# RWKV-5 attention with a tanh-shrink MLP: the upper halves of the loads issued from other queues, and a planner that counts SBUF ports

## The chip, the cores and the metric

The kernel runs on one core of a Trainium2 chip. The metric is the device time of one execution in microseconds (us); lower is better. The time before is 605.67 us, the median of three runs (603.26, 605.67 and 606.02).

## The reference

The inputs are `r`, `k`, `v` of shape (4, 8, 768, 48), that is batch, heads, sequence and head width, in float32; `w` and `u` of shape (8, 48); and two weight matrices, `w_in` (384, 2048) and `w_out` (2048, 384), which arrive in float64.

```python
state = np.zeros((B, H, D, D), dtype=np.float32)
for t in range(S):
    kt, vt, rt = (k[:, :, t], v[:, :, t], r[:, :, t])
    cur = np.einsum('bhd,bhe->bhde', u[None] * kt, vt)
    y[:, :, t] = np.einsum('bhd,bhde->bhe', rt, state + cur)
    state = w[None, :, :, None] * state + np.einsum('bhd,bhe->bhde', kt, vt)
x = y.transpose(0, 2, 1, 3).reshape(B * S, H * D)      # 3072 x 384
h = x @ w_in
g = h - np.tanh(h)
out = (g @ w_out).astype(np.float32)
```

## The kernel before

**Attention.** The recurrence is computed in chunks of 64 steps. A `unit(n)` is one chunk of two batches: the first batch lies on partitions 0 to 63, the second on partitions 64 to 127 (`HALF[0]` and `HALF[1]`). There are 24 units. Each loads its `r`, `k` and `v` in `fetch` (line 745): six DMAs, one for each tensor and each half `z`, of 64 partitions x 8 heads x 48 numbers, 96 KB in 512 runs of 192 bytes. All of these are issued by SyncE (SP) at line 750, the first half and then the second. A unit's tiles come from rings of three buffers, so that the load of unit n has to wait until unit n - 3 has been read. A unit then transposes r and k on TensorE (PE, line 763), scales them (VectorE, lines 767 and 894), multiplies them (`levels`, `from_state`, `outputs`, PE line 717), copies a masked part (VectorE, line 919) and updates the state (VectorE, lines 882 and 928). ScalarE (ACT) writes the diagonal (line 788) and the outputs `xt` and `rest` (line 855). Two units make a block of 256 tokens; when its second unit is done, GpSimd (POOL) issues six small DMAs that fill the remaining rows of `xt` from `rest` (line 876).

**Weights.** They arrive in float64, and are converted to float32 on the chip. There are 16 pieces, in turn two of `w_in` and two of `w_out`, each 768 KB in float64. `Weights.load` (line 123) brings a piece into one of four staging tiles `st`; `convert` takes five VectorE and two ScalarE instructions (lines 137 to 143). A `w_out` piece is a single SP DMA over 128 partitions. A `w_in` piece is four DMAs, because its rows are rearranged: 48 main rows (288 KB, 144 runs of 2 KB) and 16 other rows (96 KB, 48 runs) for partitions 0 to 63, and the same for partitions 64 to 127. SP issues the two main parts, POOL the two small ones.

**Dense.** There are 12 blocks of 8 tiles each. A tile is `h = x @ w_in` for 256 hidden columns (12 PE instructions, line 168), the activation (five on ScalarE, lines 177 to 185, and four on VectorE, lines 192 to 198), and the second product. For 25 tiles (24 early ones and the very last) the product is written directly (`o`, line 206). After all the weights have been converted and mixed (`mixing`, line 266), the other 71 tiles take a form with seven products instead of eight (`p`, line 257), with sums on POOL (lines 242 to 246).

**Order.** The order of instructions on every engine is not written by hand. Every step is a task of `Plan`, with an engine, a cost in us, what it comes after and, for a DMA, `data`: how long it holds the transfer channel. `forward` lays out the tasks with these costs, engine by engine, and gives a makespan. `order` searches: it starts from due times found backwards, jitters due times at random, and keeps what does not lengthen the plan; first with a plan cut off at `BUSY` us, then with the whole plan. The tasks are then issued in order of their planned start. Each engine and each DMA queue works through its own instructions in that order, so an instruction that waits holds up those behind it. A weight load is `gated`: it does not start before 9.5 us (`FIRST`) in the plan. The plan keeps a DMA off a queue that has eight in flight (`LANES`).

Of the kernel before, what the change touches and what calls it, by code (L numbers as in the profile page):

```python
# [33 lines left out]
AHEAD = 2  # L34
# [266 lines left out]
class Plan:  # L301
# [6 lines left out]

    HOP, NEAR_HOP, LANDS, LANDED, LANES, EARLY, SPARE, WARM, SLOW = 0.16, 0.06, 2.4, 1.6, 8, 45.0, 20.0, 6.0, (60.0, 3.0)
    AHEAD, BUSY = 0.05, 240.0  # L310
    CHUNK, CHUNK_0, ASKED, COMES, FIRST = 256, 192, 55, 3.4, 9.5
# [4 lines left out]

    def add(self, engine, cost, run, after=(), due=1e9, data=0, gated=False, steps=0):
        t = SimpleNamespace(engine=engine, cost=cost, run=run, after=[x for x in after if x], due=due, data=data,
                            gated=gated, steps=steps, then=[], n=len(self.tasks))
        for x in t.after:  # L320
            x.then.append(t)
        self.tasks.append(t)
        return t
# [12 lines left out]
    def forward(self, due, until=1e9):  # L336
# [3 lines left out]
        waiting = self.queues(ready, count)  # L340
        free, lanes, channel = dict(self.BEGIN), {}, 0.0
        step, bound, comes, fills = 0, self.CHUNK_0, 0.0, iter(self.fills)
# [3 lines left out]
        while len(done) < len(ready):  # L346
# [40 lines left out]
            if t.data:  # L387
                channel = max(channel, start + 1.2) + t.data
                end = max(end + self.LANDS, channel + self.LANDED) + self.slow(start)
                lanes[e] = lanes[e][1:] + [end]  # L390
# [58 lines left out]

    def order(self, first=2500, tries=500):  # L450


        due = [t.due for t in self.tasks]
        for t in reversed(self.tasks):
            for x in t.then:
                due[t.n] = min(due[t.n], due[x.n] - t.cost - self.HOP - (self.LANDS if t.data else 0))
        plan = self.forward(due)
        for _ in range(4):
            due = self.backward(plan)
            plan = self.forward(due)  # L460
        chance = Random(5)

        def moved():
            by, at, wide = chance.choice((0.3, 1, 2, 5)), chance.uniform(0, until), chance.choice((15, 40, 100, 700))
            return [x + chance.gauss(0, by) * (start is not None and abs(start - at) < wide / 2) for x, start in zip(due, plan[1])]


        until = self.BUSY
        plan = self.forward(due, until)
        for _ in range(first):  # L470
            new = moved()
            other = self.forward(new, until)
            if other[0] <= plan[0]:
                plan, due = other, new
        plan = self.forward(due)
        until = plan[0]
        for _ in range(tries):
            new = moved()
            other = self.forward(new)
            if chance.random() < .5:  # L480
                latest = self.backward(other)
                again = self.forward(latest)
                if again[0] < other[0]:
                    other, new = again, latest
            if other[0] <= plan[0]:
                plan, due = other, new
# [29 lines left out]
def near(ctx, tc, r, k, v, w, u, out, shared, moe_w_in, moe_w_out):  # L516
# [136 lines left out]
    def fills(to):  # L653
# [20 lines left out]
    doubled = add("ACT", .6, lambda: A.copy(twice, inverse[:, :, None, 1:].to_broadcast([128, NP, 2, SHORT])), [now])  # L674
    now = tabled = add("PE", .7, table, [doubled], steps=8)
    downs = add("ACT", .5, lambda: A.copy(w_down, tab.rearrange("s (h d) -> s h d", h=H)[:, :, :D]), [now])
# [6 lines left out]
        out=ub.rearrange("p h d -> p (h d)"),  # L683
        in_=bass.AP(tensor=u.tensor, offset=u.offset, ap=[[0, 128], [1, H * D]])), data=.7)

# [15 lines left out]
    for n in range(weights.count):  # L701

        queues, data = (("SP",), (3.0,)) if n % 4 > 1 else (("SP", "POOL") * 2, (1.2, .95) * 2)
        of = [add(e, .55, lambda n=n, i=i, e=e: weights.load(n, i, e_of[e]), [converted[n - 4] if n >= 4 else None],
                  data=x, gated=True) for i, (e, x) in enumerate(zip(queues, data))]
        if weights.sources[n % 4 > 1].dtype != I64:
            converted.append(of[-1])
            continue
        step = steps(lambda n=n: weights.convert(n))
        now = of + ([converted[n - 2]] if n >= 2 else [])  # L710
        for name, cost in (("DVE", .47), ("DVE", .47), ("ACT", .84), ("ACT", .84), ("DVE", .87), ("DVE", .87), ("DVE", .87)):
            now = [add(name, cost, step, now)]
        converted += now
# [7 lines left out]
    def unit(n):  # L721
# [21 lines left out]
        direct = j == 0  # L743

        def fetch(name, src, after):
            def run(z):
                if name == "k" and not hasattr(t, "kt"):
                    t.kt = first_k[slot] if direct else load.tile([128, H, D], F32, name="kt", tag="kt")
                to = {"r": rt, "v": vt}.get(name)
                Q.dma_start(out=(t.kt if to is None else to)[HALF[z], :, :D],  # L750
                            in_=src[half * 2 + z, :, steps_at, :].rearrange("h t d -> t h d"))

            of = [add("SP", .65, lambda z=z: run(z), after, data=.71) for z in range(2)]
            return add("none", 0, lambda: None, of)
# [135 lines left out]
        if two:  # L890
            free = [b1.xt, b1.rest, b1.add, b1.cp, b1.diag]
        turns, turned = .46, 16
        x.turn = add("PE", turns, lambda: turn(rt, r_ps), [x.r] + free, steps=turned)
# [9 lines left out]
        if product:  # L903
            now = add("ACT", 1.05, own_k, [x.kT, w_us])
            x.own = add("PE", .7, own_levels, [now, x.rT, b2.out], steps=64)
            x.diag = add("DVE", .64, lambda: V.copy_predicated(t.at, same.bitcast(I32)[:, None, None, :].to_broadcast([128, 2, NP, SHORT]), own_lev), [x.own, b2.out])
# [7 lines left out]
        if two:  # L914
            now = add("PE", .66, from_state, both + [x.rT, b1.xt, b1.rest, b1.add, b2.decay, x.kT], steps=64)
            begun = [add("ACT", .15, between, [now])]
        x.lev = add("PE", .7 if two else (1.33 if swap else 1.73) if ch else .7, levels,
                    begun + [x.kT, x.rT, b2.out] + ([b2.decay, b1.xt, b1.rest, b1.add] if ch else []), steps=128 if ch and not two else 64)
        x.cp = add("DVE", .64, lambda: V.copy_predicated(t.at, before, lev), [x.lev, b2.out] + ([] if product else [x.diag]))  # L919
        x.out = now = add("PE", .95 if direct else 1.21, outputs,  # L920
                          [x.cp, x.diag, x.v, b1.xt, b1.rest, b1.add] + ([x.extra] if direct else [x.kw]), steps=96 if direct else 128)
        if direct:
            now = x.out = add("PE", .55, to_state, [now, x.kw], steps=64)
        x.xt = add("ACT", .96 if swap else .4, to_xt, [now, last_h.get(j - FIRST - 2) if slot == 0 else None])
        if not direct:
            x.rest = add("ACT", .62 if swap else .26, to_rest, [x.xt] + (filled.get((j - 2, "all"), []) if slot == 0 else []))
        x.add = add("DVE" if ch else "ACT", .47 if ch else 1.2, keep, [x.out, x.rest, x.xt]) if more else None
        x.decay = x.add if not ch else add("DVE", .47, lambda: V.tensor_tensor(state[:, :, :, :D], state[:, :, :, :D], w_all, ALU.mult), [x.add]) if more else None
        if direct:
            filled.setdefault((j, "all"), []).append(x.xt)  # L930
        elif slot == L - 1:
            filled[j, "all"] = [add("POOL", .52, lambda i=i, kk=kk: fill(i, kk), [x.rest, x.xt], data=.1)
                                for kk in range(NK) for i in range(2)]
# [17 lines left out]
    def finished_seven(t, x, half, due, pace):  # L951
# [9 lines left out]
        for i in (1, 0):  # L961
            now = steps[4 if i else 6]
            if t.fs[0]:
                now = add("DVE", .47, lambda i=i: dense.gather(t, i), [now], due + 3 * pace)
            stored[j, i] = [add("POOL", .6, lambda z=z, i=i: dense.store(t.os[i], L * j + i, z, G), [now], due + 4 * pace, data=.4)
                            for z in range(2)]

    def hidden(j, fs, f, due, pace, seven=False):
# [40 lines left out]
        for i in range(L):  # L1009
# [7 lines left out]
            if whole and j < d.NB - 1:  # L1017

                stored[j, i] = [add("POOL", .6, lambda z=z, i=i, ends=ends: dense.store(ends.o, L * j + i, z, G),
                                    [x.empty[-1]], due + 4 * pace, data=.4) for z in range(2)]  # L1020

# [339 lines left out]
```

## Time and profile before

| What | Value |
|---|---|
| median of three runs | 605.67 us |
| profiled execution | 607.26 us |
| its span, first to last instruction | 605.5 us |
| mean granted TensorE clock | 0.989 |
| TensorE busy | 582.4 us (96%) |
| VectorE busy | 466.4 us (77%) |
| ScalarE busy | 403.3 us (67%) |
| GpSimd busy | 201.0 us (33%) |
| packets of the DMA queue of SP (q1) | 81084, 25.57 MB |
| packets of the DMA queue of POOL (q0) | 4992, 6.99 MB |

The page of a profile splits the span into 40 slices of 15.1 us, and gives for each engine a digit for its busy share in tenths. The chain of work that ended last is followed back from the last instruction through whatever released each step. A table of windows gives the busy time of an engine in stretches that one chooses, the granted clock, the mean share of the time for which the 16 DMA engines had a packet under way, and the rate at which bytes moved. The name SPq means the sequencer of SP, which does no work but issue DMAs. Matmul ends are modelled, so a busy TensorE may still be fed slowly.

### The profile page before, as it was taken

The numbers are of one execution on the slowest core, as the hardware profiler recorded it, in microseconds if no ns is written. First come the engines' busy times: TensorE is split into PE (matmuls) and PEld (weight loads), VectorE is DVE, ScalarE is ACT, GpSimd is POOL, SyncE is SP. The second block draws the span as 40 slices with busy tenths as digits, with TensorE's granted clock in tenths as the row PEclk, the third lists the DMA queues.
The fourth block names the chain that finished last, engine by engine and source line by source line (L and its number), as shares of the span: only waits on it lengthen the run. The fifth ranks groups of instructions, "written<-read, shape, count | busy, mean of one in ns | idle before, by whom it ended". The sixth has DMA issues, their size and how long they took to land.

```text
span 605.5 us, 14670 instructions
## 1 busy us (share of the span) xinstructions
PE 582.4 (96%) x5781; PEld 485.7 (80%) x5781; DVE 466.4 (77%) x782; ACT 403.3 (67%) x902; POOL 201.0 (33%) x366
## 2 busy tenths in 40 slices
PE   8877999999999999999999999999999999999996
PEld 4555767667777669999999999888889889889995
DVE  6699699999999999867677776767765775555666
ACT  3677699899866676655556686465866676565652
POOL 5002212021000123544455473425334435334540
PEclk9889899999999999999999999999999999999999
DMA  6966585967300210110111020122201100100101
GB/s 125 228 126 126 113 194 99 143 167 124 105 14 0 48 28 14 26 27 1 28 27 26 2 60 1 41 41 48 53 16 34 41 2 8 29 2 8 26 3 30
DMA packets 86326, 33.78 MB, mean 56 GB/s; under 512 B 78536, under 2 KB 80680, under 8 KB 86248
## 3 DMA queue, kind: packets, MB, share of 16 engines
q1 hardware_dynamic: 81084, 25.57, 21.1%
q0 software_dynamic: 4992, 6.99, 5.5%
q8 instruction: 47, 0.77, 0.5%
q14 instruction: 31, 0.25, 0.2%
q10 hardware_dynamic: 172, 0.20, 0.1%
HBM read 26.94 MB, written 4.72 MB: 52 GB/s over the span
## 4 chain that ended last, share of the span: by engine, by line
PE 76%; DVE 6%; DMA 5%; ACT 4%; issue 4%; SPq 3%; POOL 1%; DVEq 0%; ACTq 0%; POOLq 0%
PE h L168 37%; PE p L257 26%; PE o L206 6%; PE yk_ps L717 4%; SPq L750 3%; DMA st<-in_moe_w_in_dram 2%; DMA xt<-rest 1%; PE yk_ps L763 1%; POOL xt L876 1%; DMA st<-in_moe_w_out_dram 1%; DVE rT L767 1%; DVE at L919 1%; ACT s L177 1%; DVE tg L194 1%; DVE g L198 1%
## 5 line engine op out<-in xcount | busy, mean ns | idle before, releaser
L168 PE MATMUL h<-xt,w_in_sb 128*128 128x256 f32 x1152 | 285.7, 385 | 2.7 <-DMA xt<-rest 2.7
L168 PEld LDWEIGHTS h<-xt,w_in_sb 128*128 128x128 f32 x1152 | 214.6, 192 | 35.9 <-issue 2.1
L242 POOL TENSOR_TENSOR sg<-g 128x256 f32<-128x256 f32 x69 | 52.1, 755 | 176.7 <-DVE g L198 152.2
L257 PE MATMUL p<-mixed,sg 128*128 128x192 f32 x426 | 104.1, 326 | 0.0
L192 DVE TENSOR_TENSOR g<-h,th 128x512 f32<-128x512 f32 x96 | 65.8, 686 | 48.9 <-ACT s L177 23.0
L194 DVE SCALAR_TENSOR_TENSOR tg<-s,tg 128x512 f32<-128x512 f32 x96 | 71.1, 741 | 36.6 <-ACT tg L181 20.0
L181 ACT ACTIVATE tg<-h 128x512 f32<-128x512 f32 x96 | 57.2, 596 | 58.5 <-PE h L168 56.9
L179 ACT ACTIVATE th<-h 128x512 f32<-128x512 f32 x96 | 57.4, 598 | 39.1 <-PE h L168 39.0
L177 ACT ACTIVATE s<-h 128x512 f32<-128x512 f32 x96 | 57.4, 598 | 37.3 <-PE h L168 37.2
L876 POOL DMA_DIRECT2D xt<-rest x66 | 32.5, 499 | 146.3 <-ACT rest L855 145.8
L257 PEld LDWEIGHTS p<-mixed,sg 128*128 128x128 f32 x426 | 75.0, 190 | 0.3 <-issue 0.3
L198 DVE COPY_PREDICATED g<-small,tg 128x512 f32<-128x512 int32 x96 | 71.1, 741 | 4.7 <-DVE tg L196 0.5
L257 PE MATMUL p<-w_out_sb,g 128*128 128x192 f32 x284 | 71.9, 335 | 1.1 <-DVE at L919 1.1
L196 DVE SCALAR_TENSOR_TENSOR tg<-q,tg 128x512 f32<-128x512 f32 x96 | 67.5, 703 | 6.4 <-ACT q L183 2.4
L206 PE MATMUL o<-w_out_sb,g 128*128 128x384 f32 x192 | 71.3, 495 | 0.1
L183 ACT ACTIVATE q<-s,m1b 128x512 f32<-128x512 f32 x96 | 69.8, 727 | 0.6
L185 ACT ACTIVATE small<-s,smallb 128x512 f32<-128x512 f32 x96 | 69.6, 725 | 0.3
L257 PEld LDWEIGHTS p<-w_out_sb,g 128*128 128x128 f32 x284 | 51.8, 190 | 9.0 <-DVE at L919 1.5
L788 ACT ACTIVATE at<-same,du 128x64 f32<-128x64 f32 x184 | 47.9, 343 | 2.8 <-DVE du L784 2.6
L206 PEld LDWEIGHTS o<-w_out_sb,g 128*128 128x128 f32 x192 | 35.2, 190 | 15.8 <-DVE g L198 0.2
L246 POOL TENSOR_TENSOR sg<-sg,g 128x128 f32<-128x128 f32 x69 | 41.0, 594 | 5.1
L244 POOL TENSOR_TENSOR sg<-sg,g 128x128 f32<-128x128 f32 x69 | 36.6, 530 | 5.2
(133 smaller groups left out, 672.3 us busy)
## 6 DMA issues: line engine op xcount, KB each, us to landing
st<-in_moe_w_out_dram SPq DMA_DIRECT2D x8, 768.0 KB, 4.5
rt<-in_r_dram SPq DMA_DIRECT2D x48, 96.0 KB, 2.9
vt<-in_v_dram SPq DMA_DIRECT2D x48, 96.0 KB, 3.4
st<-in_moe_w_in_dram SPq DMA_DIRECT2D x16, 288.0 KB, 5.5
kt<-in_k_dram SPq DMA_DIRECT2D x44, 96.0 KB, 3.1
out_dram<-o POOLq DMA_DIRECT2D x44, 96.0 KB, 2.2
st<-in_moe_w_in_dram POOLq DMA_DIRECT2D x16, 96.0 KB, 6.0
xt<-rest POOLq DMA_DIRECT2D x66, 16.0 KB, 2.1
```

The lines of the kernel that those rows point to most:

```text
L168: self.nc.tensor.matmul(t.h2[:, z], self.w_in_sb[:, t.f // 2, kk, z * 128 : (z + 1) * 128], self.xts[t.j][:, kk].rearrange("p b t -> p (b ...
L177: A.activation(out, t.h, AF.Square)
L179: A.activation(out, t.h, AF.Tanh)
L181: A.activation(out, t.h, AF.Tanh, scale=G1)
L183: A.activation(out, t.s, AF.Square, bias=self.m1b)
L185: A.activation(out, t.s, AF.Relu, bias=self.smallb, scale=-1.0)
L192: V.tensor_tensor(t.g, t.h, t.th, ALU.subtract)
L194: V.scalar_tensor_tensor(t.tg, t.s, C4, t.tg, ALU.mult, ALU.mult)
L196: V.scalar_tensor_tensor(t.tg, t.q, K1, t.tg, ALU.add, ALU.mult)
L198: V.copy_predicated(t.g, t.small.bitcast(I32), t.tg)
L206: self.nc.tensor.matmul(self.outs[i], t.g2[:, z, i * C : (i + 1) * C], self.w_out_sb[:, t.f + z, :], start=t.first and z == 0, stop=t.last ...
L257: self.nc.tensor.matmul(ps[bank][:, half * n : (half + 1) * n], a, b, start=t.first and half == 0, stop=t.last, skip_group_check=True)
```

## The change

It has two parts.

The first moves DMAs between queues. Of a `w_in` piece, the main rows for partitions 64 to 111 go from SP to POOL, and the small part for partitions 112 to 127 from POOL to SP. Of the loads of r, k and v, the second batch (partitions 64 to 127) is issued by ACT for units 0 and 1, by POOL for units 2 to 11, and by SP as before from unit 12 on.

The second changes the planner. A task with `side` 0 or 1 also occupies a port group for 1.75 times its channel time; every queue has its own ring; many costs are given other numbers; the first search is cut off at 110 us instead of 240, and is done four times with 2000 tries, of which the best is kept; the search over the whole plan has 300 tries instead of 500. Since the order of every engine comes out of this search, it can differ everywhere.

```diff
-    HOP, ..., LANDS, LANDED, LANES, EARLY, SPARE, WARM, SLOW = 0.16, 0.06, 2.4, 1.6, 8, 45.0, 20.0, 6.0, (60.0, 3.0)
-    AHEAD, BUSY = 0.05, 240.0
+    HOP, ..., LANDS, LANDED, LANES, EARLY, SPARE, WARM, SLOW = 0.16, 0.06, 2.1, 1.35, 8, 45.0, 20.0, 6.0, (60.0, 1.5)
+    AHEAD, BUSY, STARTS = 0.05, 110.0, 4
+    HALF = 1.75
...
             if t.data:
-                channel = max(channel, start + 1.2) + t.data
-                end = max(end + self.LANDS, channel + self.LANDED) + self.slow(start)
+                begin = max(start + 1.4, ring.get(e, 0.0))
+                channel = max(channel, begin) + t.data
+                ring[e] = channel
+                if t.side is not None:
+                    ports[t.side] = max(ports[t.side], begin) + self.HALF * t.data
+                    ring[e] = max(channel, ports[t.side])
+                end = max(end + self.LANDS, ring[e] + self.LANDED) + self.slow(start)
...
-    def order(self, first=2500, tries=500):
+    def order(self, first=2000, tries=300):
...
-        for _ in range(first):
-            new = moved()
...
+        until, begun, best = self.BUSY, due, None
+        for _ in range(self.STARTS):
+            due = begun
+            plan = self.forward(due, until)
+            for _ in range(first):
...
+            if best is None or plan[0] < best[0]:
+                best = plan[0], due
+        due = best[1]
...
-        queues, data = (("SP",), (3.0,)) if n % 4 > 1 else (("SP", "POOL") * 2, (1.2, .95) * 2)
+        queues, data, sides = (("SP",), (2.5,), (None,)) if n % 4 > 1 else (("SP", "POOL", "POOL", "SP"), (.82, .4, .82, .4), (0, 0, 1, 1))
...
+        def queue(z):
+
+            return "SP" if not z else "ACT" if n < 2 else "POOL" if n < 12 else "SP"
...
-                Q.dma_start(out=(t.kt if to is None else to)[HALF[z], :, :D],
+                e_of[queue(z)].dma_start(out=(t.kt if to is None else to)[HALF[z], :, :D],
...
-            of = [add("SP", .65, lambda z=z: run(z), after, data=.71) for z in range(2)]
+            of = [add(queue(z), .65, lambda z=z: run(z), after, data=.28, side=z) for z in range(2)]
...
-        turns, turned = .46, 16
+        turns, turned = .38, 16
...
-        x.lev = add("PE", .7 if two else (1.33 if swap else 1.73) if ch else .7, levels,
+        x.lev = add("PE", .6 if two else (1.06 if swap else 1.46) if ch else .56, levels,
...
-        x.out = now = add("PE", .95 if direct else 1.21, outputs,
+        x.out = now = add("PE", .86 if direct else .97, outputs,
```

More of the change, by code (lines that the diff above doesn't have):

```diff
@@ L301 @@
 class Plan:
-    HOP, NEAR_HOP, LANDS, LANDED, LANES, EARLY, SPARE, WARM, SLOW = 0.16, 0.06, 2.4, 1.6, 8, 45.0, 20.0, 6.0, (60.0, 3.0)
-    AHEAD, BUSY = 0.05, 240.0
+    HOP, NEAR_HOP, LANDS, LANDED, LANES, EARLY, SPARE, WARM, SLOW = 0.16, 0.06, 2.1, 1.35, 8, 45.0, 20.0, 6.0, (60.0, 1.5)
+    AHEAD, BUSY, STARTS = 0.05, 110.0, 4
+    HALF = 1.75
     CHUNK, CHUNK_0, ASKED, COMES, FIRST = 256, 192, 55, 3.4, 9.5
@@ L315, in __init__, with add @@
         self.tasks, self.fills = [], []
-    def add(self, engine, cost, run, after=(), due=1e9, data=0, gated=False, steps=0):
+    def add(self, engine, cost, run, after=(), due=1e9, data=0, gated=False, steps=0, side=None):
         t = SimpleNamespace(engine=engine, cost=cost, run=run, after=[x for x in after if x], due=due, data=data,
-                            gated=gated, steps=steps, then=[], n=len(self.tasks))
+                            gated=gated, steps=steps, side=side, then=[], n=len(self.tasks))
         for x in t.after:
@@ L340, in forward @@
         waiting = self.queues(ready, count)
-        free, lanes, channel = dict(self.BEGIN), {}, 0.0
+        free, lanes, channel, ring, ports = dict(self.BEGIN), {}, 0.0, {}, [0.0, 0.0]
         step, bound, comes, fills = 0, self.CHUNK_0, 0.0, iter(self.fills)
@@ L465, in moved @@
             return [x + chance.gauss(0, by) * (start is not None and abs(start - at) < wide / 2) for x, start in zip(due, plan[1])]
-        until = self.BUSY
-        plan = self.forward(due, until)
-        for _ in range(first):
-            new = moved()
-            other = self.forward(new, until)
-            if other[0] <= plan[0]:
-                plan, due = other, new
+        until, begun, best = self.BUSY, due, None
[3 more added lines that the diff above has]
+            for _ in range(first):
+                new = moved()
+                other = self.forward(new, until)
+                if other[0] <= plan[0]:
+                    plan, due = other, new
+            if best is None or plan[0] < best[0]:
+                best = plan[0], due
+        due = best[1]
         plan = self.forward(due)
@@ L674, in near @@
     doubled = add("ACT", .6, lambda: A.copy(twice, inverse[:, :, None, 1:].to_broadcast([128, NP, 2, SHORT])), [now])
-    now = tabled = add("PE", .7, table, [doubled], steps=8)
+    now = tabled = add("PE", .5, table, [doubled], steps=8)
     downs = add("ACT", .5, lambda: A.copy(w_down, tab.rearrange("s (h d) -> s h d", h=H)[:, :, :D]), [now])
@@ L683, in near @@
         out=ub.rearrange("p h d -> p (h d)"),
-        in_=bass.AP(tensor=u.tensor, offset=u.offset, ap=[[0, 128], [1, H * D]])), data=.7)
+        in_=bass.AP(tensor=u.tensor, offset=u.offset, ap=[[0, 128], [1, H * D]])), data=.5)
     add("ACT", 1.3, lambda: A.activation(fixed("warm", [128, 1]), shared["one"], AF.Tanh), due=0)
@@ L701, in near @@
     for n in range(weights.count):
-        queues, data = (("SP",), (3.0,)) if n % 4 > 1 else (("SP", "POOL") * 2, (1.2, .95) * 2)
+        queues, data, sides = (("SP",), (2.5,), (None,)) if n % 4 > 1 else (("SP", "POOL", "POOL", "SP"), (.82, .4, .82, .4), (0, 0, 1, 1))
         of = [add(e, .55, lambda n=n, i=i, e=e: weights.load(n, i, e_of[e]), [converted[n - 4] if n >= 4 else None],
-                  data=x, gated=True) for i, (e, x) in enumerate(zip(queues, data))]
+                  data=x, gated=True, side=side) for i, (e, x, side) in enumerate(zip(queues, data, sides))]
         if weights.sources[n % 4 > 1].dtype != I64:
@@ L903, in unit @@
         if product:
-            now = add("ACT", 1.05, own_k, [x.kT, w_us])
-            x.own = add("PE", .7, own_levels, [now, x.rT, b2.out], steps=64)
+            now = add("ACT", 1.2, own_k, [x.kT, w_us])
+            x.own = add("PE", .5, own_levels, [now, x.rT, b2.out], steps=64)
             x.diag = add("DVE", .64, lambda: V.copy_predicated(t.at, same.bitcast(I32)[:, None, None, :].to_broadcast([128, 2, NP, SHORT]), own_lev), [x.own, b2.out])
@@ L914, in unit @@
         if two:
-            now = add("PE", .66, from_state, both + [x.rT, b1.xt, b1.rest, b1.add, b2.decay, x.kT], steps=64)
+            now = add("PE", .58, from_state, both + [x.rT, b1.xt, b1.rest, b1.add, b2.decay, x.kT], steps=64)
             begun = [add("ACT", .15, between, [now])]
-        x.lev = add("PE", .7 if two else (1.33 if swap else 1.73) if ch else .7, levels,
+        x.lev = add("PE", .6 if two else (1.06 if swap else 1.46) if ch else .56, levels,
                     begun + [x.kT, x.rT, b2.out] + ([b2.decay, b1.xt, b1.rest, b1.add] if ch else []), steps=128 if ch and not two else 64)
         x.cp = add("DVE", .64, lambda: V.copy_predicated(t.at, before, lev), [x.lev, b2.out] + ([] if product else [x.diag]))
-        x.out = now = add("PE", .95 if direct else 1.21, outputs,
+        x.out = now = add("PE", .86 if direct else .97, outputs,
                           [x.cp, x.diag, x.v, b1.xt, b1.rest, b1.add] + ([x.extra] if direct else [x.kw]), steps=96 if direct else 128)
         if direct:
-            now = x.out = add("PE", .55, to_state, [now, x.kw], steps=64)
+            now = x.out = add("PE", .5, to_state, [now, x.kw], steps=64)
         x.xt = add("ACT", .96 if swap else .4, to_xt, [now, last_h.get(j - FIRST - 2) if slot == 0 else None])
@@ L926, in unit @@
             x.rest = add("ACT", .62 if swap else .26, to_rest, [x.xt] + (filled.get((j - 2, "all"), []) if slot == 0 else []))
-        x.add = add("DVE" if ch else "ACT", .47 if ch else 1.2, keep, [x.out, x.rest, x.xt]) if more else None
+        x.add = add("DVE" if ch else "ACT", .47 if ch else .95, keep, [x.out, x.rest, x.xt]) if more else None
         x.decay = x.add if not ch else add("DVE", .47, lambda: V.tensor_tensor(state[:, :, :, :D], state[:, :, :, :D], w_all, ALU.mult), [x.add]) if more else None
@@ L931, in unit @@
         elif slot == L - 1:
-            filled[j, "all"] = [add("POOL", .52, lambda i=i, kk=kk: fill(i, kk), [x.rest, x.xt], data=.1)
+            filled[j, "all"] = [add("POOL", .52, lambda i=i, kk=kk: fill(i, kk), [x.rest, x.xt], data=.1, side=i)
                                 for kk in range(NK) for i in range(2)]
@@ L964, in finished_seven @@
                 now = add("DVE", .47, lambda i=i: dense.gather(t, i), [now], due + 3 * pace)
-            stored[j, i] = [add("POOL", .6, lambda z=z, i=i: dense.store(t.os[i], L * j + i, z, G), [now], due + 4 * pace, data=.4)
+            stored[j, i] = [add("POOL", .6, lambda z=z, i=i: dense.store(t.os[i], L * j + i, z, G), [now], due + 4 * pace, data=.3)
                             for z in range(2)]
@@ L1019, in hidden @@
                 stored[j, i] = [add("POOL", .6, lambda z=z, i=i, ends=ends: dense.store(ends.o, L * j + i, z, G),
-                                    [x.empty[-1]], due + 4 * pace, data=.4) for z in range(2)]
+                                    [x.empty[-1]], due + 4 * pace, data=.3) for z in range(2)]
     for n in range(L * (FIRST + 2)):
```

## The prediction

> **What bounds the kernel now.** I read the digits by slice first, then tables of windows, then the chain of waits in the stretch that they pointed to.
>
> ```profile
> PE   8877999999999999999999999999999999999996
> DVE  6699699999999999867677776767765775555666
> GB/s 125 228 126 126 113 194 99 143 167 124 105 14 0 48 28 14 26 27 1 28 27 26 2 60 1 41 41 48 53 16 34 41 2 8 29 2 8 26 3 30
> ```
>
> The digits show two regimes. Up to about slice 15 (228 us) VectorE is at nines; from there TensorE alone is. Loads move in the first eleven slices (166 us). The second table gives VectorE (DVE) by stage; its columns are the window, its length, the busy time, the granted clock, the DMA share and GB/s.
>
> ```profile
> 0.00:20.00 20.00, 11.25 (x26) 1.00 0.79 133
> 20.00:60.00 40.00, 36.61 (x62) 0.91 0.77 160
> 60.00:135.00 75.00, 67.23 (x116) 0.96 0.73 144
> 135.00:228.00 93.00, 90.14 (x148) 1.00 0.25 53
> 228.00:605.00 377.00, 261.16 (x434) 1.00 0.11 24
> ```
>
> VectorE idles for 8.75, 3.39, 7.77 and 2.86 us in the four stages before 228, 22.8 in all. After 228 TensorE is busy for 372.7 of 377 us (same table for all engines). So I take the work after 228 as a fixed load: the end moves by as much as the first stages get shorter, and these can hardly get shorter by more than the idle time of VectorE. That is the cap on the whole change, 22.8 us, unless work moves from before 228 to after it.
>
> Why is VectorE idle? The chain of waits (start, length, what) and the list of waits (total, times, longest) name loads:
>
> ```profile
> 10.94 8.65 DMA st<-in_moe_w_in_dram
> 27.13 3.43 SPq L750
> 34.97 2.36 DMA kt<-in_k_dram
> 52.54 6.17 DMA xt<-rest
> ```
>
> ```profile
> DVE power L137 <- DMA st<-in_moe_w_in_dram: 2.9, 1, 2.9
> ```
>
> Between 2.11 and 10.9 us the chain is SP issuing, one load every 0.68 us; then it is the first weight piece, 19.6 us at its landing; from 25.7 to 37.3 SP again. SP's own timeline shows what is wrong with the latter:
>
> ```profile
> 13.42 5.89 SPq L750 DMA_DIRECT2D kt<-in_k_dram  x2
> 22.91 4.17 SPq L750 DMA_DIRECT2D rt<-in_r_dram  x2
> 27.13 4.35 SPq L750 DMA_DIRECT2D kt<-in_k_dram  x2
> ```
>
> Two such issues normally take 1.3 us. Here they take 4 to 6: [...] 10.5 us lost over the three.
>
> [...] the columns are again window, length, clock, DMA share, GB/s.
>
> ```profile
> 4.00:9.00 5.00, 1.00 0.72 145
> 13.00:19.00 6.00, 1.00 1.14 165
> 24.00:28.00 4.00, 0.84 0.98 339
> ```
>
> At 24 to 28 us a `w_out` piece over 128 partitions moves 339 GB/s with engines at 0.98; at 13 to 19 us the half-height `w_in` parts move 165 GB/s with the engines just as full (1.14). At 4 to 9 us the engines are not full: 96 KB every 0.68 us is 145 GB/s, which is SP's issuing alone. [...] At 4 to 9 us that is just what is scarce. [...] no row of this trace has both halves' main parts on two queues at once, so it stays open. [...]
>
> **The change, part by part.**
>
> *r, k, v of units 0 and 1 to ACT.* Six issues leave SP's first thirteen: 6 x 0.68 = 4.1 us. ACT gets six, at SP's 0.64 each 3.8 us; it is busy 7.83 of the first 20 us, and what queues behind them are the copies of the decay tables (5.3 to 8.5 us). Bounds: nothing if they fall into its gaps, +1 us if a copy on the decay chain is pushed back. I take 0. Unit 0 itself gains nothing, since its kT at 8.59 us waits for the reciprocal, not for loads; unit 1's k, which VectorE awaits until 13.65, comes some 3 us earlier.
>
> *w_in's halves on two queues.* SP and POOL have the main parts for the two halves in flight together. From 9.5 us on (the gate), 1.4 us to start and 1.3 to land (my split of about the shortest landing of a load, 2.5 us), and 768 KB at 265 GB/s (the rate of 20 to 30 us) to 339 = 2.3 to 3.0 us: 14.5 to 15.2, say 15.5 with unit 1's rest in the way, against 19.6. That is 4.1 us earlier. If the halves serialize after all, it is the 19.6 less only the cleared traffic, about 18.5. VectorE has 4.7 us idle between 10 and 20 us (10 less 5.27 in that window); I credit 3.2 of it. The 1.5 kept are waits for TensorE (1.35 before line 919).
>
> *r, k, v of units 2 to 11 to POOL.* Thirty issues leave SP: 30 x 0.65 = 19.5 us, plus its holds. They are not a saving in themselves: buffers of three units still set when they may start (SP waited 24.1 us for line 763 before 135 us). In 20 to 60 us VectorE has only 3.39 us to give, and I credit 1.0; between 60 and 135 us it has 7.77, of which I put 2.07 at 61.5 and 2.19 at 66.0 down to the late `xt` fill of 58.7 (TensorE waited for it and VectorE for TensorE); I credit 2.8.
>
> What a POOL load costs is unknown. POOL's issues in the trace (min/median/max ns):
>
> ```profile
> L123 POOL DMA_DIRECT2D st<-in_moe_w_in_dram x16: 510/523/836, 9.2 to 145.7; - x16
> L876 POOL DMA_DIRECT2D xt<-rest x66: 484/484/839, 50.1 to 547.8; - x66
> L295 POOL DMA_DIRECT2D out_dram<-o x44: 521/540/566, 250.2 to 570.1; - x44
> ```
>
> They have 48, 16 and 64 runs: 56 ns for 48 more runs, 1.17 ns each. A load of 512 runs is then 484 + 496 x 1.17 = 1.06 us, an estimate eight times beyond the data. [...] At 1.06, 30 loads are 32 us; POOL is busy 4.5 of 20 to 60 and 15.5 of 60 to 135 us, so it has room. What queues behind a POOL load that waits for its buffer are the six fills of `xt` and two weight parts; the fills are on the chain at 50 to 58.7 us. The eight small parts moved to SP cost it 8 x 0.44 us and the eight main parts leave it: even.
>
> *The planner.* It does no work on the chip. Its effect is the order; against what is done now that can be a gain or a loss, and I bound it by 3 us either way, about one such wait as TensorE's longest at present (3.1 before line 763, for kw). Value taken: 0.
>
> *Sum.* 3.2 + 1.0 + 2.8 = 7.0 us. The profiled execution took 607.26 us (span 605.5, 1.8 around it) and would take 600.3; it lies 1.6 above the median, so against the median 605.67 the forecast is 598.7, given as **598.5**.
>
> **The rivals.**
>
> *Rival 1, VectorE was the bound anyway (14%).* The digits are nines from 20 us on. Then only the first weight piece counts, and what it brings is partly lost in the queue of converts behind it: 1 to 2 us, about 604. For it: 97% busy in 135 to 228 us. Against: the idle times of 8.75 us before 20 and 7.77 us after 60.
>
> *Rival 2, slower: POOL's loads are dear (15%).* [...] Before 60 us SP loaded 8 units, from unit 2 at about 12 us: 48 us for six, 8 us each. Three loads per unit on POOL fit if one costs less than 8 / 3 = 2.7 us; that is where it decides. At 3.0 us a unit takes 9, ten units are 10 us late, and 3.5 of the gains at the front remain: +6.5, about 612. For it: no such load in this trace. Against: the 1.17 ns per run.
>
> *Rival 3, only the order counts (15%).* The queues turn out to serialize, and the result is the new plan's order, 605.7 plus or minus 3.
>
> The main case has 56%. Its own range is 592 to 602.5.
>
> **How the numbers follow.** A measurement of this kernel can tell about 0.5%, 3 us, from no change. Faster by more: 0.54 of the main case, 0.04 of rival 1, 0.03 of rival 2 (a small loss at POOL, the rest kept), 0.05 of rival 3: 0.66. Within: 0.02 of the main case, 0.09 of rival 1, 0.04 of rival 3: 0.15. Slower: 0.01, 0.12 and 0.06 of the rivals: 0.19. The range takes in the planner's gain on top of the main case (590) and rival 2 (612).
>
> **What would show each step.** Right: the first conversion (line 137) starts before 16.5 us; POOL's r, k, v issues last 0.6 to 1.5 us; SP's pairs no longer last over 4 us; VectorE is above 93% busy from 20 to 135 us; the seven-product tiles (line 257) begin about 7 us earlier than 228. Wrong: the first conversion at 18 us or later (halves serialize); POOL issues above 2.7 us, with TensorE waiting for `xt<-rest` or kt; or VectorE's idle time falling while its first 257-tile does not move.

## The result and the profile after

The changed kernel takes 603.69 us (median of 20 runs, 601.16 to 604.85) where the kernel before took 605.13 on the same chip: a ratio of 0.996, with a 95% interval of 0.9944 to 0.9976. By that ratio it is 2.4 us faster, 1.5 to 3.4 by the interval, where the two medians alone lie 1.4 us apart; the forecast was 7. The profiled execution took 604.56 us, its span 602.4 (before: 607.26 and 605.5).

In the digits by slice of the changed kernel, VectorE (DVE) dips in the third slice (30 to 45 us), where it was at nine, and no longer in the fifth (60 to 75 us), where it was at six:

```profile
PE   7579999999999999999999999999999999999996
...
DVE  5679999999999999998788775686874855663866
...
GB/s 128 184 155 142 129 164 111 145 163 75 50 86 27 60 29 21 34 20 28 27 26 27 1 27 1 41 41 47 28 40 35 41 2 9 28 1 8 26 3 30
```

The table of windows for VectorE after (window, length, busy time, granted clock, DMA share, GB/s) puts numbers to it:

```profile
0.00:20.00 20.00, 11.78 (x27) 0.91 0.81 134
20.00:60.00 40.00, 29.57 (x51) 0.83 0.86 161
60.00:135.00 75.00, 71.89 (x124) 1.00 0.62 144
135.00:228.00 93.00, 91.55 (x148) 1.00 0.26 55
228.00:602.00 374.00, 269.56 (x436) 1.00 0.11 23
```

Up to 228 us VectorE idles for 8.22, 10.43, 3.11 and 1.45 us, 23.2 in all, against 22.8 before. The idle time did not shrink; it moved. The stage from 60 to 135 us gained 4.7 us, that from 20 to 60 us lost 7.0. Accordingly the first seven-product tile (line 257) starts at 225.8 us, against 227.0 before. The rest of the 3.1 us between the two spans lies after it: 376.6 us from that tile to the end, against 378.5.

The chain of waits (start, length, what) and VectorE's list of waits from 23 to 42 us (total, times, longest) name loads again. Most line numbers of the attention are 12 to 16 higher after the change: the fetch is at 766, kw at 910, rk at 796.

```profile
14.07 13.93 DMA st<-in_moe_w_in_dram
...
30.83 9.20 DMA rt<-in_r_dram
```

```profile
DVE kw L910 <- DMA kt<-in_k_dram: 4.1, 1, 4.1
DVE rk L796 <- DMA rt<-in_r_dram: 3.0, 1, 3.0
```

And SP's timeline shows it held for longer than before, although half of these loads are gone from its queue. Counting every issue of over 1 us between 9.5 and 60 us and taking 0.6 off for each, SP was held for 18.6 us over 28 issues, before for 11.1 us over 50:

```profile
17.82 10.43 SPq L766 DMA_DIRECT2D kt<-in_k_dram  x1
...
32.40 3.47 SPq L766 DMA_DIRECT2D kt<-in_k_dram  x1
```

One issue of 96 KB took 10.4 us. All four first weight pieces had been requested by 16.3 us, on both queues, ahead of the rest of unit 3's loads, and what came behind waited. The windows (window, length, clock, DMA share, GB/s) show the engines full:

```profile
13.00:19.00 6.00, 1.00 1.16 164
28.00:36.00 8.00, 0.75 1.15 225
```

From 13 to 19 us, with the main parts on two queues, 164 GB/s are moved. Before, with the main parts on SP alone, it was 165.

### The profile page after: what moved, and what is told of

Its sections match the earlier page's. It is cut to its first block, busy times and chain, and to the rows that moved or that the text cites. A ratio compares the mean times of both kernels' runs of the same rounds, so it can differ in the third digit from the quotient of the medians.

```text
span 602.4 us, 14669 instructions
## 1 busy us (share of the span) xinstructions
PE 580.1 (96%) x5779; PEld 484.6 (80%) x5779; DVE 474.3 (79%) x782; ACT 403.9 (67%) x902; POOL 228.4 (38%) x396
## 4 chain that ended last, share of the span: by engine, by line
PE 80%; DVE 7%; DMA 5%; issue 3%; ACT 2%; POOL 2%; ACTq 0%; DVEq 0%; POOLq 0%
PE h L168 38%; PE p L257 25%; PE o L206 8%; PE yk_ps L729 5%; DMA rt<-in_r_dram 2%; DMA st<-in_moe_w_in_dram 2%; PE x_ps L779 1%; PE yk_ps L779 1%; DVE g L192 1%; PE x_ps L729 1%; DMA xt<-rest 1%; DVE tg L196 1%; DVE tg L194 1%; DVE state L898 1%; PE p L206 0%
## 5 line engine op out<-in xcount | busy, mean ns | idle before, releaser
L194 DVE SCALAR_TENSOR_TENSOR tg<-s,tg 128x512 f32<-128x512 f32 x96 | 74.4, 775 | 35.4 <-ACT tg L181 24.7
L192 DVE TENSOR_TENSOR g<-h,th 128x512 f32<-128x512 f32 x96 | 65.8, 686 | 36.3 <-ACT s L177 18.6
L196 DVE SCALAR_TENSOR_TENSOR tg<-q,tg 128x512 f32<-128x512 f32 x96 | 70.2, 732 | 4.9 <-ACT q L183 1.3
L246 POOL TENSOR_TENSOR sg<-sg,g 128x128 f32<-128x128 f32 x69 | 43.9, 636 | 4.9
L244 POOL TENSOR_TENSOR sg<-sg,g 128x128 f32<-128x128 f32 x69 | 40.3, 584 | 4.9
```

What stands on the lines that cost most here:

```text
L192: V.tensor_tensor(t.g, t.h, t.th, ALU.subtract)
L194: V.scalar_tensor_tensor(t.tg, t.s, C4, t.tg, ALU.mult, ALU.mult)
L196: V.scalar_tensor_tensor(t.tg, t.q, K1, t.tg, ALU.add, ALU.mult)
```

## The experiments

Ratios are to the kernel before, measured on the same chip in the same session, with 95% intervals. Each planned kernel is one draw of a random search.

### The order without the queues, and the queues without the order

The plan and what it issues can be separated: the plan may believe in one queue while the instruction goes to another.

```diff
 x1 (from the kernel after)
-  e_of[queue(z)].dma_start(out=(t.kt if to is None else to)[HALF[z], :, :D],
+  Q.dma_start(out=(t.kt if to is None else to)[HALF[z], :, :D],
   and weights.load(n, i, e_of[("SP", "POOL")[i % 2]])
 x2 (from the kernel before): the opposite at the same two places
 x3 (from the kernel after)
+  e_of["SP" if n < 2 else queue(z)].dma_start(...)
```

> The changed kernel with the order of its own planner, but every DMA issued by the queue that issued it before (r, k, v all by SP; w_in's main parts by SP, its small ones by POOL). Theory 'order': the 2.4 us come from the new order and the queues give nothing, so this stays at 0.996 of the kernel before, within 0.3%. Theory 'queues': the new queues bring the gain of 6.9 us between 60 and 135 us, so without them this is at or above the kernel before (1.000 to 1.012), SP being short of issue time: 96 loads of 0.65 us in an order that was planned for 60.

Measured: 601.99 us, **0.9936** [0.9919, 0.9953].

> The kernel before with the order of its own planner, but every DMA issued by the queue that issues it after the change. Theory 'queues': 4 to 7 us faster than before (0.988 to 0.993), since the loads come earlier in an order that suited them. Theory 'order': within 0.3% of before. Rival 'ACT': ACT's six loads stand in front of its copies for the decay tables[...], so the front is 1 to 2.5 us later: 1.000 to 1.004.

Measured: 606.48 us, **1.0018** [0.9999, 1.0037].

> The changed kernel in its own order, with the six loads that ACT issues (units 0 and 1, second batch) issued by SP instead. Theory 'ACT costs the front': the decay copies on ACT (w_up at 9.22 us, 6.70 before) come 1.5 to 2.5 us earlier and the end 1 to 2 us earlier than in the changed kernel (0.993 of before). Rival 'weights crowd the loads': the front is set by the weight pieces that are all asked for by 16.3 us, so the end stays within 0.2% of the changed kernel (0.996).

Measured: 603.36 us, **0.9951** [0.9933, 0.9969].

The new order on the old queues is at least as good as the whole change (0.9936 against 0.996), and the new queues under the old order bring nothing. So the gain is the order's. Giving only ACT's six loads back to SP (x3) comes out 0.1% below the whole change, with intervals that overlap: at this order they cost next to nothing, not the 1 to 2 us of the first theory. SP is held under the old order and new queues as well; from the timeline of x2:

```profile
17.59 10.82 SPq L750 DMA_DIRECT2D kt<-in_k_dram  x1
```

### The loads by themselves

Three kernels hold only loads, in groups with a barrier between, and measure the rate of each kind. Each was executed once. The first two are these:

```diff
+ small(S, S, 8); small(S, P, 8); small(S, A, 8)        # r, k, v: 8 pairs of halves by SP+SP, SP+POOL, SP+ACT
+ small(S, P, 8, same=True); small(P, P, 8)             # both into one half; POOL alone
+ wide((S, S), 4, (0, 2)); wide((S, P), 4, (0, 2))      # w_in's main parts, 4 pairs
+ wide((S, P), 4, (0, 2), same=True); full(4)           # both into one half; w_out
...                                                     # whole w_in pieces: queues of before, of after
```

> This kernel leaves out all of the computation: it only issues groups of loads, one group after the other, each waiting for the one before, and writes zeros. Groups: eight pairs of 96 KB r/k/v loads with the two halves (partitions 0 to 63, 64 to 127) on SP and SP, on SP and POOL, on SP and ACT, and on SP and POOL with both of a pair on partitions 0 to 63; then four pairs of 288 KB w_in main parts on SP and SP, on SP and POOL, and on SP and POOL to the same lower half; four 768 KB w_out pieces on SP; four whole w_in pieces with the queues of before (SP, POOL, SP, POOL), with those of after, and with those of after and the two main parts issued first; eight r/k/v pairs on POOL alone. Theory 'ports' (that of the prediction): [...] SP and POOL moves the w_in main parts at 1.6 to 2 times the rate of SP and SP, and the same-half group does not. Rival 'engines': the 16 DMA engines are already full with one queue, so all three w_in groups run at the same rate within 15%, about 165 to 200 GB/s. For r/k/v: if issuing is the limit, SP and SP runs at 145 GB/s and SP and POOL at 1.5 to 2 times that; rival: within 20%. [...] SP and ACT gains less than SP and POOL.

Measured: 196.06 us, but the groups were not separate: POOL's loads of a group began before the group ahead was through, so its rates by group say nothing. The next kernel makes POOL wait at each barrier.

> Like the first kernel of loads alone (all computation left out), but with every group held back until the one before has landed on all queues, which the first did not do for POOL. From the first: SP and SP moved the four pairs of w_in main parts at 177 GB/s with engines full (share 1.00), w_out 356 GB/s. Theory 'ports': SP and POOL to two halves at 280 GB/s or more, to the same half 177. Rival 'engines': 177 to 205 in both, that is, less than 15% for the second queue. For r/k/v pairs: 'issue' theory, 16 loads take 13.4 us on SP alone and 8 us on SP and POOL; rival, 11 to 12 us. SP and ACT no better than 12 us[...]; POOL alone 13 to 14 us.

Measured (one execution, 217.23 us), from the windows of the packets (window, length, clock, DMA share, GB/s): r, k, v by SP and SP, then by SP and POOL; w_in's main parts by SP and SP, by SP and POOL, and by SP and POOL into one half.

```profile
3.30:14.70 11.40, 1.00 0.75 138
28.80:38.20 9.40, 1.00 1.17 167
...
86.00:99.70 13.70, 1.00 1.00 172
101.70:113.70 12.00, 1.00 0.99 197
115.80:131.00 15.20, 1.00 1.01 155
```

From first issue to last landing the four w_in pairs took 15.43 us on SP alone, 13.77 on two queues, 17.09 into one half. A second queue made the halves faster by 1.12, not by two; which half was written did matter, since sending both into one cost 1.24 against separate ones. The r, k, v groups took 13.15 us by SP alone, where issuing seems to limit them (138 GB/s is one load of 96 KB every 0.71 us, and SP took 0.68 for an issue in the kernel before; the engines' share is 0.75), 12.74 by POOL alone, 11.78 with SP and POOL, 11.74 with SP and ACT and 12.16 with both into one half. Whole w_in pieces, four of them, took 18.81 us on the queues of before and 17.26 on those of after: 1.5 us for four pieces. Even that hangs on the order of issue: on the same new queues, but with both main parts issued ahead of the small ones, it was 18.76.

In this kernel no issue of SP took over 0.75 us, although the engines' share was 0.99 to 1.01 in all the groups of w_in's main parts. Full engines alone did not hold SP there.

The third kernel asks what makes these loads slow: their height or the length of their runs.

```diff
+ narrow(4, (S, S), 2); narrow(4, (S, P), 2)   # w_out's rows of 3 KB, in halves
+ tall(4); flat(4)                       # w_in over 128 partitions in one DMA, runs of 2 KB and of 6 KB
+ tall_small(8)                          # r, k, v over 128 partitions in one DMA
```

> Loads alone again (all computation left out), group after group: four w_out pieces over 128 partitions (3 KB runs); the same bytes as two half-height DMAs each, both on SP; the same on SP and POOL; four 768 KB pieces of w_in over 128 partitions in runs of 2 KB; the same in runs of 6 KB; eight r/k/v loads over 128 partitions in one DMA of 1024 runs of 192 bytes; eight pairs of half-height ones on SP. What made w_in's main parts slow (172 GB/s against 354 for w_out, engines full in both)? Theory 'half height' (the prediction's): w_out at half height on SP drops to 170 to 220 GB/s, and w_in at full height in 2 KB runs reaches 300 or more. Rival 'the source': w_in's rows, 2 KB out of 16 KB, are slow to read whatever the height: w_in at full height stays below 220, and w_out at half height stays above 300.

Measured (one execution, 126.41 us): w_out whole, w_out in halves by SP and SP, in halves by SP and POOL, and w_in whole in 2 KB runs:

```profile
12.60:22.90 10.30, 1.00 0.89 305
28.90:42.80 13.90, 1.00 0.98 226
45.10:57.70 12.60, 1.00 0.99 249
59.80:69.10 9.30, 1.00 0.97 338
```

The runs are not what slows w_in: 2 KB runs over 128 partitions move at 338 GB/s. Cutting a transfer into two of 64 partitions does, for w_out too (305 to 226; whole, it moved 358 in the kernel before this one), and a second queue wins back only a tenth (249). The cut also halves the size of each DMA; that the height does it and not the size was not tried apart. For r, k and v full height does not help: one DMA over 128 partitions moved 156 GB/s, no more than two halves on two queues (167). They differ from the fast transfers in their runs, 192 bytes against 2 and 3 KB, and in their size, 192 KB against 768; which of the two counts was not tried apart. In this group SP was held: its first two issues of 1024 runs took 0.38 and 0.58 us, each later one 1.14 to 1.20 us, about the 1.26 us that 192 KB last at 156 GB/s. So SP was held here where many short runs were queued.

### The planner's draw and the planner

```diff
 y1, z3: before with Random(6), Random(7);  z1: after with Random(6)
-  chance = Random(5)
+  chance = Random(6)
 y2 (from before): BUSY = 110.0, STARTS = 4, order(first=2000, tries=300) and its loop, nothing else
 y3 (from after; z2 the same with Random(6)): changed planner, planned for and issued on the old queues
-  ("SP", "POOL", "POOL", "SP"), (.82, .4, .82, .4), (0, 0, 1, 1)
+  ("SP", "POOL") * 2, (.82, .4, .82, .4), (0, 0, 1, 1)
-  return "SP" if not z else "ACT" if n < 2 else "POOL" if n < 12 else "SP"
+  return "SP"
```

> The kernel before with another seed of its planner's random search, nothing else. This measures what a mere redraw of the order is worth. Theory 'the new planner's model matters': within 0.3% of before (0.997 to 1.003). Rival 'dice': the gain of the new order (0.994 with old queues) is within what a redraw gives, so this may be anywhere in 0.99 to 1.01, and is off by more than 0.4%.

Measured: 604.25 us, **0.9958** [0.994, 0.9977].

> The kernel before with a third seed. The two draws so far are 1 and 0.9958. Theory 'dice': between 0.992 and 1.004. If it is below 0.992, a redraw alone covers everything seen so far.

Measured: 606.68 us, **0.9999** [0.9978, 1.002].

> The kernel before with the search settings of the changed kernel alone (first search cut off at 110 us, four starts of 2000, then 300 tries), and the old costs and transfer model. Theory 'search': 0.994 to 0.996, since the search aims at the stretch where the gain was. Rival 'costs': the gain comes from the new costs, so this is within 0.3% of before.

Measured: 606.04 us, **0.9977** [0.9953, 1.0].

> The changed planner, numbers and search, told the truth about the old queues: every load of r, k, v on SP, w_in's main parts on SP. Theory 'order': as fast as the changed order put on the old queues or faster, 0.990 to 0.994, since it was made for these queues. Theory 'the plan needs relief of SP': slower than that, 0.998 to 1.005, since the plan sees SP's queue full and starts work later.

Measured: 599.74 us, **0.9879** [0.9842, 0.9916].

> The changed kernel with another seed of the planner's search, queues as changed. Theory 'dice': a redraw moves it as it moved the kernel before (0.4%): anything from 0.988 to 1.000 of before. Theory 'model': stays within 0.2% of the changed kernel, 0.994 to 0.998.

Measured: 602.04 us, **0.9944** [0.9924, 0.9963].

> The changed planner planned for the old queues (which measured 0.988 of before) with another seed. Theory 'the new planner is good, the queues cost': 0.987 to 0.992, clear of both draws of the kernel before (1 and 0.996) and below the redraw of the changed kernel. Theory 'dice': 0.993 to 0.998.

Measured: 598.91 us, **0.9873** [0.9841, 0.9904], the fastest of all here.

One other draw moves the kernel before by 0.4%, as much as the whole change does. So a single comparison of two planned kernels can't tell 0.4%. But the two draws of the changed planner on the old queues (0.988, 0.987) lie clear of the two draws of the change (0.996, 0.994) and of the three of the kernel before: **on the old queues the changed planner is worth some 7 us, and planned for the moved queues 4 to 5 of them are gone.** The issuing itself is the smaller part of that loss. With the order kept, going back to the old queues gained 1.5 us (x1 against the kernel after) and taking the new ones lost 1.1 (x2 against the kernel before), both at the edge of what their intervals tell. The rest lies in the order that the planner makes when it counts on the moved queues.

VectorE from 20 to 135 us in y3:

```profile
20.00:60.00 40.00, 34.14 (x59) 0.91 0.84 175
60.00:135.00 75.00, 73.56 (x126) 1.00 0.68 137
```

The first seven-product tile starts at 221.4 us. The gain from 60 to 135 us is here as well, and the loss from 20 to 60 is smaller. But where VectorE idles is largely a matter of the draw, as its busy time in the two stages, its idle time up to 228 us and the ratio show:

| Kernel | Queues | busy, 20 to 60 us | busy, 60 to 135 us | idle up to 228 us | Ratio |
|---|---|---|---|---|---|
| before | old | 36.6 | 67.2 | 22.8 | 1 |
| y1, before redrawn | old | 34.1 | 70.1 | 20.1 | 0.996 |
| z3, before redrawn | old | 32.9 | 70.3 | 21.6 | 1.000 |
| after | moved | 29.6 | 71.9 | 23.2 | 0.996 |
| z1, after redrawn | moved | 35.4 | 71.9 | 19.9 | 0.994 |
| x1, order of after | old | 32.3 | 70.9 | 21.8 | 0.994 |
| y3, planned for these queues | old | 34.1 | 73.6 | 18.3 | 0.988 |
| z2, y3 redrawn | old | 32.8 | 73.1 | 19.3 | 0.987 |

Two mere redraws of the kernel before have some 3 of the 4.7 us that the change gained from 60 to 135 us. And z1, with the moved queues, loses 1.2 us from 20 to 60 and not 7.0, although it too had asked for its first four weight pieces early, by 17.9 us. So neither that loss nor that gain can be put down to the queues from the trace of one draw.

### One move at a time, each planned for

```diff
 from y3
 a1: queues of a w_in piece ("SP", "POOL", "POOL", "SP"), the rest as y3
 a2: return "SP" if not z or n < 2 else "POOL" if n < 12 else "SP"
 a3: return "SP" if not z else "ACT" if n < 2 else "SP"
```

> The changed planner with r, k, v all on SP, and only w_in's parts on the new queues, planned so. Alone on the chip a w_in piece took 4.3 us with the new queues, 4.7 with the old. Theory 'w_in is harmless': 0.985 to 0.990 of before, as with the old queues. Rival 'w_in costs': 0.992 to 0.996.

Measured: 599.75 us, **0.9883** [0.9864, 0.9902].

> The changed planner with w_in on its old queues and only the second batch of units 2 to 11 on POOL, planned so. Theory 'POOL is the cost': 0.992 to 0.996 (loads on POOL wait in line with the fills of xt and each other, and the plan takes two queues for twice the rate, where loads alone gained a tenth). Rival: 0.986 to 0.990.

Measured: 607.62 us, **1.0031** [1.0014, 1.0049].

> The changed planner with only the six loads of units 0 and 1 on ACT, planned so. Theory 'ACT is the cost': the decay copies on ACT stand behind loads [...], 1.5 to 2.5 us at the front, 0.990 to 0.993. Rival 'ACT costs nothing that remains': 0.986 to 0.989.

Measured: 604.33 us, **0.9963** [0.9942, 0.9983].

Moving w_in's halves is harmless. POOL's r, k, v cost 1.5% against y3 and ACT's 0.8%; both are more than any redraw made here (0.4%), but each is a single draw. They do not add up either: together they would be 2.3%, where the changed kernel, with all three moves, is 0.8 to 0.9% behind y3 and z2. So they are what a queue and the plan made for it cost together, and not prices of a queue. In a2, VectorE's windows from 20 to 135 us, and two waits of TensorE from there:

```profile
20.00:60.00 40.00, 33.40 (x58) 0.88 1.01 189
60.00:135.00 75.00, 66.41 (x114) 0.98 0.61 126
```

```profile
PE h L168 <- DMA xt<-rest: 3.7, 1, 3.7
PE x_ps L779 <- DMA rt<-in_r_dram: 3.0, 2, 2.1
```

VectorE loses 7.2 us against y3 from 60 to 135 us, and TensorE, before 60 us, waits for an `xt` fill and for r. The fills requested from 50.2 us on landed up to 7.2 us later, with SP's and POOL's own loads in flight beside them. That is not much more than in the kernel before (up to 6.4 us) or y3 (up to 6.2), so late fills alone do not explain the loss; its cause is not shown. In a3 the loss is at the front, 9.03 us busy in the first 20 against 11.21 in y3, and VectorE waits for unit loads:

```profile
DVE rk L796 <- DMA rt<-in_r_dram: 4.8, 1, 4.8
```

### Which part of the planner

```diff
 from y3
 a4: begin/ring/ports taken out, channel and LANDS as before, data costs of before, no side
 a5: PE and ACT costs of before (turns .46, levels .7 to 1.73, outputs .95 and 1.21, ...), transfers as y3
```

> The changed planner's compute costs and search, the old queues, and the transfer model of the kernel before (0.71 for 96 KB, one channel, no ports). Theory 'compute costs make the gain': 0.986 to 0.990. Rival 'the transfer model makes it': 0.996 to 1.000.

Measured: 604.32 us, **0.9963** [0.9948, 0.9979].

> The changed planner's transfer model and search with the earlier kernel's compute costs, everything on the earlier queues. If the compute costs carry the part of the planner's gain that the transfer model with its absence left over (0.996 against 0.988), the ratio to the kernel before lies between 0.992 and 0.998. If the transfer model does it alone, it is 0.987 to 0.991, and the compute costs matter to nothing.

Measured: 602.49 us, **0.9938** [0.9912, 0.9964].

Neither alone gives the 0.988. The transfer model with the new search gives 0.994, the compute costs with the new search 0.996, the new search alone 0.998 (y2). With redraws worth 0.4%, and one draw of each, the two shares can't be divided more finely.

## Why the prediction was right or wrong

**The sum, term by term.** The prediction credited VectorE with 3.2 us before 20 us, 1.0 from 20 to 60, 2.8 from 60 to 135, and took 0 for the planner. In the profiled executions 0.5 came before 20 us, 7.0 were lost from 20 to 60, and 4.7 came from 60 to 135; with 1.4 from 135 to 228 us, the idle time was as long as before. Three steps failed: the rate of two halves on two queues, the worth of a second issuer for r, k and v, and the 0 for the planner.

**What bounds it: held in the main.** From the first seven-product tile to the end it took 375.6 to 381.2 us in all sixteen planned kernels, while that tile's start ranged from 218.1 to 230.3. The end did follow the first stages, though not one for one: the earliest start (z1) has the longest rest and the latest (a2) the shortest. The cap of 22.8 us was not exceeded by any (the largest gain in span was 7.3).

**w_in's halves on two queues: the rate was wrong.** The term was 768 KB at 265 to 339 GB/s, the rates of windows in which w_out's full-height piece was moving. Two half-height parts on two queues did not add up to one full-height transfer: whole pieces alone moved at 199 GB/s between their first packet and their last (17.26 us for four, from the first issue to the last landing), and 197 is the rate of the main parts. The first conversion starts at 19.21 us (before 19.71) where 15.5 was forecast, so the credit of 3.2 us was a credit of half a microsecond. This is the prediction's own sign "18 us or later". Nor does an earlier first conversion show up at the end: in a1, with only these parts moved, it starts at 17.6 us, in y3 at 20.0, and the two times agree (0.9883 and 0.9879). Half height was slow in the runs (226 against 305 GB/s for the same w_out data), and on two queues both parts into one half took 1.24 times as long as into separate halves (17.09 against 13.77 us). That both halves at once would then reach the full rate was the author's estimate, and no row of the trace before showed it. A second queue brought 10% (w_out, 226 to 249 GB/s) and 14% (w_in, 172 to 197): the two streams did not quite serialize, but they came nearer to that than to the full rate (305 and 338).

**r, k, v of units 2 to 11 to POOL: no gain of theirs.** The price was over-estimated. The group of POOL's issues after (min, median, max ns) reads

```profile
L766 POOL DMA_DIRECT2D kt<-in_k_dram x10: 682/683/716, 12.2 to 80.9; - x10
```

0.68 us where 1.06 was estimated; rival 2, which needed 2.7, is out by its own price. But a second issuer did not relieve SP: with 22 issues fewer before 60 us it was held for longer, once for 10.4 us. What holds SP is not settled; it went with full engines (a share of 1.06 over the issue of 10.4 us) and many short runs queued (the 1.14 to 1.20 us of the third kernel of loads), and not with the number of its own issues. The credit of 1.0 us from 20 to 60 us became a loss. The 2.8 us from 60 to 135 us did come, by luck: x1 has 3.7 of the 4.7 with the old queues, and two redraws of the kernel before have 2.9 and 3.1. The prediction feared for the fills of `xt` queued behind a POOL load. In a2 the late fills did not stand in such a line: POOL had been idle for 1.45 us, waiting for ACT's `rest`, before it issued them. Alone and planned for, this part costs 1.5%. How much of that is POOL's queue and how much the order planned around it was not separated for this part; for the whole change, x1 against after gives 0.24% for the queues at a given order, with intervals that overlap.

**r, k, v of units 0 and 1 to ACT: taken at 0, open.** Planned alone it cost 0.8%, 5 us, in its one draw; VectorE had done 2.2 us less than in y3 after the first 20. In the order of the changed kernel it cost 0.1% (x3), less than can be told. What it does to the front can be seen. In the changed kernel's chain ACT stands behind a landing:

```profile
2.52 5.28 DMA rt<-in_r_dram
7.83 0.60 ACTq L766
```

ACT's second group of loads started at 7.83 us, just after a first one had landed at 7.80; SP stood still from 5.06 to 8.29 us, and the profile puts 3.2 us of that down to the landing of a load. By 5.06 us SP had issued six DMAs and ACT four. The planner counts eight places in flight for each queue (`LANES`), so by its count neither had to wait. In the kernel before, SP issued 13 DMAs in a row up to 10.23 us and did not wait for a landing. The first kernel of loads has the same: beside POOL, SP issued its eight loads in a row, one every 0.68 us, but with ACT as the second queue each of the two issued four and then paused, SP for 1.23 us and ACT for 1.60. So a second queue on ACT did not let SP go on with its own issues as one on POOL did. Why is not shown. The copies of the decay tables behind it came late too: w_up began at 9.22 us, in x3 at 8.2 and before at 6.70. VectorE waited 0.8 us for it.

**The planner: the term taken at 0 was the largest one.** Bounded by 3 us either way, it is worth some 7 on the old queues. Rival 3, "only the order counts", had the mechanism. That its range of 602.7 to 608.7 holds the result is in part luck, since 4 to 5 of those 7 us went again in the plan for the moved queues. Rival 1, about 604, also names the measured time, but its ground, that VectorE had no more to give, does not hold: y3 and z2 end 6.3 and 7.3 us earlier in span, with 18.3 and 19.3 us idle up to 228 us instead of 22.8.

Why a plan with the changed transfer costs is better stays open. They are not more exact: a w_in piece costs 2.4 us of the channel in the new plan and 4.3 in the old, and measured 4.3 to 4.7 alone; a pair of r loads 0.56 against 1.42, and measured 1.5 to 1.6. Nor was it tried what the plan does differently with loads that it thinks cheap.

## What to carry to other kernels

A DMA queue that was held while the engines' share was at 1 (SP for 10.4 us at 1.06) was here no sign of too few issuers: before moving loads to another queue, measure one group of them alone on one and on two queues, and look first at whether a transfer can be made full height (w_out moved 305 GB/s whole and 226 in halves; in this kernel that was not tried for w_in). Where a plan counts places in flight for each queue, look in the timeline at whether a second queue stops together with the first (here SP from 5.06 to 8.29 us, and ACT until 7.83). And where a search writes the order, redraw its random numbers before believing a difference of half a per cent, or reading a cause from where one draw idles, and test a change of queues and a change of planner apart.

## What the runs showed of the hardware that was not expected

- The share of busy DMA engines did not tell a slow transfer from a fast one: it was 0.98 at 226 GB/s (half height, one queue), 0.99 at 249 (half height, two queues) and 0.97 at 338 (full height).
- A DMA of 512 runs of 192 bytes occupied POOL for 0.68 us, only 0.2 us more than one of 16 runs (0.48); the slope of 1.17 ns per run read from three short kinds did not continue.
- SP's issue of a load stretched from 0.6 us to 10.4 and 10.8 us (the kernel after and x2), yet with the engines' share at 1.00 and loads of 144 runs it stayed under 0.75 (the second kernel of loads). With loads of 1024 runs in a row it settled at 1.14 to 1.20 (the third).
- ACT was as good a second queue as POOL for r, k and v alone (11.74 and 11.78 us), yet inside the kernel ACT's second group of loads started only at 7.83 us, after a load had landed at 7.80, and SP stood still until 8.29.
